# Code products of two halves in one score tile, and three PSUM banks shared by hash, transpositions and row sums

## The chip, the cores and the metric

One core of one Trainium2 chip runs the kernel. The metric is the time of one execution in device microseconds; three runs of the kernel before gave 784.03, 784.47 and 784.84 us, a median of 784.47.

## The reference

Three networks follow each other. The first is attention with a mask by hashes: batch 2, 8 heads, 768 positions, 64 columns a head, and six hash bits a position.

```
q_bits = (q @ proj > 0)            # proj: 64 x 6
k_bits = (k @ proj > 0)
mask = bucket(q_bits) == bucket(k_bits)
scores = where(mask, q @ k.T / 8, -1e9)
attn = softmax(scores)             # along the keys
x = attn @ v                       # then heads side by side: 1536 x 512
x = (sigmoid(x @ w_gate) * (x @ w_val)) @ w_out         # d_ff 1536
h = x @ w_in                                             # d_ff 2048
out = where(h >= 1, h, where(h <= -1, 0, (h + 1)^2 / 4)) @ w_out2
```

## The kernel before

The change is in the attention stage. It works on eight pairs of heads, `(b, p)`, one after the other; the two heads of a pair have `e` = 0 and 1. A pair has twelve units (6 blocks of 128 queries x 2 heads).

**A unit.** `QK` on TensorE makes 128 x 768 scores in a score tile `sc` of two PSUM banks; there are two such tiles (four banks). The mask is inside this product: beside q and k the operands hold a code of the hash bits, so a pair of another bucket gets a large negative score. Four tiles an operand, called `U`, `W`, `H` and `N` (first word of the number, rest, and the two that take codes), carry values of one head and codes of the other in their two halves of 64 partitions. `MAX` on VectorE takes the row maximum, `EXP` on ScalarE writes the probabilities `P` in SBUF and releases the score tile.

**Transpositions.** Two units give three `T`: four 128 x 128 transpositions on TensorE into one bank `pt`. `HI` (ScalarE) and `LO` (VectorE) read it out as two float16 words `PT`; `LO` releases the bank. There are two `pt` banks. `PV` multiplies `PT` by v into the bank `pv`, as two column tiles of 64, in three pieces a group of two blocks. The row sums go from `rb` through `R` (a transposition into a `pt` bank) and `RSC` (`rs`, ScalarE) into `EV`, which scales the result.

**The next pair's operands** (class `Prep`). While a pair runs, the next is prepared. GpSimd scales q and splits q and k (`SCL`, `TOP`, `RST`: tiles `U` and `W`). `Z` on TensorE makes the 24 hash products of both sides and both halves of the positions, in four groups of 32 partitions, in the bank `mm`; `BITS` (ScalarE) makes them +1 or -1 in `bt`. `XP` is a product of a code matrix with `bt`, for q or k (j) and a half of 384 positions (n): `code4[:, g]` holds the code in the 32 rows of its group and zeros in the others, so all 128 rows are used. Each of the four `XP` goes into the bank `mm`, and `H` (ScalarE, lines 406 and 408) makes codes of 384 columns in tile `N` from it. Six DMA copies an operand (`copy`, line 448, on SyncE's queue) move half tiles to the other 64 partitions; `H<-N` and `N<-W` are the last, and `N<-W` waits until `H<-N` has read `N`.

**The order** is written out as numbers. Table `AT` is for the first and the last pair and `AM` for the six between; a number is a place in units, twelve to a pair, and all steps are sorted by it and then recorded. Each engine, and SyncE's queue, takes them in that order. Tiles are taken from their pools in that order too: a step may stand only behind those that release what it takes. The weights of the gated network (`a_load`, three DMAs of 1 MB together) and their conversion to float32 have places in it as well.

The first pair has its own preparation ahead of the table (`first_round`); there the code products use 32 rows each (`part=True`). After attention the two gated networks run in one list; TensorE multiplies without a pause there.

Of the kernel before, what the change touches and what calls it, by code (L numbers as in the profile page):

```python
# [29 lines left out]
def lsh_attention_glu_act(ctx, tc, qt, kt, v, proj, w_gate, w_val, w_out1, w_in2, w_out2, ident_d, code_d, out):  # L30
# [27 lines left out]
    code4 = const.tile([128, 4, 128], BF16, name="code4")  # L58
# [3 lines left out]
    def constants():  # L62
        nc.gpsimd.memset(pz, 0.0)
        for e, r in ((0, E), (1, O)):
            nc.scalar.dma_start(pz[r, e * NB:(e + 1) * NB], proj[r])
        nc.scalar.dma_start(code, code_d)
        nc.vector.memset(bt, 0.0)
        nc.gpsimd.memset(code4, 0.0)
# [242 lines left out]
    SCB, PVB, MMB, PTB = 2, 1, 1, 2  # L311
    PB = {"pt": PTB, "pv": PVB, "mm": MMB}
# [4 lines left out]
    def bank(nm, tag):  # L317
        return pA.tile([128, 512], F32, tag=tag, bufs=PB[tag], name=nm)
# [16 lines left out]
    with ExitStack() as actx:  # L335
# [18 lines left out]
        class Prep:  # L354
# [6 lines left out]
            def part(self, n):  # L361
                return slice(0, S) if n is None else slice(n * HN, (n + 1) * HN)

            def bank(self, n, name):
                if n is None:
                    return sc_tile(name)[:, :, 0:HN]
                return pA.tile([128, 512], F32, tag="mm", bufs=MMB, name=f"{name}_{n}")[:, 0:HN]

            def sb(self, t, n):
                return v2(t) if n is None else t[:, self.part(n)]  # L370

# [9 lines left out]
            def z(self):  # L381

                self.z_ps = pA.tile([128, 512], F32, tag="mm", bufs=MMB, name=f"z_{self.b}_{self.p}")
# [53 lines left out]
            def H(self, j, n=None):  # L437
                self.x_ps = self.XB.pop((j, n))
                self.Hot(j, self.t4[j][3], slice(0, 128), n)
# [53 lines left out]
        class Flip:  # L493
            def __init__(self, n):
# [3 lines left out]
                self.ps = [None] * PCS  # L498

            def T(self, m):  # L500
                self.ps[m] = pA.tile([128, 4, 128], F32, tag="pt", bufs=PTB, name=f"pt_{self.n}_{m}")
# [79 lines left out]
        with tc.manual_schedule():  # L581
# [31 lines left out]
            load_qk(*seq[1], nc.sync)  # L613
            nc.sync.dma_start(ident, ident_d)
# [31 lines left out]
            xk = [pA.tile([128, 512], F32, tag="pt", bufs=PTB, name=f"xk_{n}")[:, 0:HN] for n in range(2)]  # L646
            for j in range(2):
                for a in range(2):
                    pp.codes(xk[a] if j else xq[:, a, 0:HN], j, a, True)
            for dst, r in ((3, E), (2, O)):  # L650
# [22 lines left out]
                "XP": (3.74, 4.91, 5.72, 7.78),  # L673
                "H": (4.54, 5.60, 7.69, 8.77),
# [12 lines left out]
                "QK": (-1.5699, -0.1016, 0.0682, 0.9466, 0.5520, 4.0360, 2.0477, 3.1663, 5.6055, 7.9530, 7.9537, 9.5136),  # L687
                "MAX": (-1.1746, 0.0191, 0.4586, 1.8498, 1.1111, 4.7351, 3.1347, 4.1102, 5.8048, 9.2404, 8.7297, 9.9059),
                "EXP": (-0.0309, 0.1949, 0.6555, 2.9824, 1.8225, 4.9578, 3.1946, 4.6720, 7.3708, 9.8795, 9.2945, 10.2827),
# [710 lines left out]
```

## Time and profile before

| | |
|---|---|
| time, median of 3 runs | 784.47 us (784.03 to 784.84) |
| time of the profiled execution | 784.46 us |
| its span | 782.7 us, 13018 instructions |
| TensorE busy | 764.4 us, 98% |
| VectorE, ScalarE, GpSimd busy | 626.5, 522.4, 169.3 us |
| mean granted clock of TensorE | 0.997 of full speed |

In the rows PE is TensorE and PEld its weight loads, DVE VectorE, ACT ScalarE, POOL GpSimd, and SPq SyncE's queue of DMAs. Busy shares are means over stages: VectorE is busy nine tenths in the first 250 us, where attention runs, and six tenths at the end. TensorE has no stage in which it is seldom busy. Matmuls are pipelined and their ends are modelled; so what one costs is read from its start to the next one's start, and a wait from the idle time in square brackets. A releaser named there is the last one that the profile saw; a DMA can have been later.

### The profile page before, as it was taken

What the parts mean: (1) busy time and instruction counts of PE and PEld (TensorE: products, weight loads), DVE (VectorE), ACT (ScalarE), POOL (GpSimd) and SP (SyncE); (2) the same over time, 40 slices, a digit from 0 to 9 for tenths busy, and PEclk for the clock granted to TensorE, in tenths of its full rate; (3) what the DMA queues carried; (4) which work ended last, traced back from release to release, by engine and by line L of the source; (5) the groups of instructions that cost most, each with busy time, mean ns of one, the idle gap of its engine ahead of it and who ended that gap; (6) DMA issues with size and microseconds to landing.
All of it is one profiled execution on the core that took longest, in us unless ns stands there. A gap on an engine that the chain in (4) does not pass through costs nothing.

```text
span 782.7 us, 13018 instructions
## 1 busy us (share of the span) xinstructions
PE 764.4 (98%) x4880; PEld 689.4 (88%) x4880; DVE 626.5 (80%) x1091; ACT 522.4 (67%) x1026; POOL 169.3 (22%) x173
## 2 busy tenths in 40 slices
PE   7999998999999999999999999999999999999997
PEld 4777876887888999999999999998998998899986
DVE  6989997989987978778769958878988867666643
ACT  6988887989875565565564544456667567766753
POOL 7656487576595000000000000000000000000000
PEclk9999999999999999999999999999999999999999
DMA  7754456354201113122122422433233201000002
GB/s 215 187 133 131 104 148 189 83 142 111 54 1 54 54 63 100 54 69 94 55 80 81 135 82 64 140 120 106 90 103 107 81 0 69 14 1 0 1 1 80
DMA packets 41391, 66.49 MB, mean 85 GB/s; under 512 B 5744, under 2 KB 28656, under 8 KB 41328
## 3 DMA queue, kind: packets, MB, share of 16 engines
q1 hardware_dynamic: 40592, 64.97, 28.4%
q8 instruction: 38, 0.62, 0.3%
q10 hardware_dynamic: 736, 0.69, 0.3%
q14 instruction: 25, 0.20, 0.1%
HBM read 45.58 MB, written 3.15 MB: 62 GB/s over the span
## 4 chain that ended last, share of the span: by engine, by line
PE 66%; DVE 1%; ACT 0%; issue 0%; ACTq 0%
PE qa L292 3%; PE qa L293 3%; PE qa L291 3%; PE p L293 3%; PE p L291 3%; PE p L292 3%; PE y L293 2%; PE qb L291 2%; PE y L292 2%; PE y L291 2%; PE qe L291 2%; PE qe L293 2%; PE qe L292 2%; PE qb L292 2%; PE qb L293 2%; PE qa L1159 2%
## 5 line engine op out<-in xcount | busy, mean ns | idle before, releaser
L517 DVE SCALAR_TENSOR_TENSOR PT<-pt,PT 128x512 f16<-128x512 f32 x144 | 95.5, 684 | 11.0 <-ACT PT L514 7.6
L478 DVE TENSOR_REDUCE st<-sc 128x1 f32<-128x768 f32 x96 | 90.9, 948 | 9.2 <-PE sc L470 8.5
L514 ACT ACTIVATE PT<-pt 128x512 f16<-128x512 f32 x144 | 81.8, 601 | 21.2 <-PE pt L505 20.3
L482 ACT ACTIVATE P<-sc,st 128x768 f32<-128x768 f32 x96 | 87.1, 908 | 8.7 <-DVE st L478 7.7
L505 PE MATMUL pt<-ident,P 128*128 128x128 f32 x576 | 80.8, 278 | 4.6 <-DVE PT L517 3.2
L505 PEld LDWEIGHTS pt<-ident,P 128*128 128x128 f32 x576 | 66.0, 141 | 14.9 <-DVE PT L517 8.2
L562 PE MATMUL O<-PT,vh 128*64 128x256 f16 x576 | 54.8, 278 | 0.0
L293 PE MATMUL p<-yh,whl_i 128*128 128x384 f32 x128 | 42.9, 336 | 0.0
L291 PE MATMUL p<-yh,whl_i 128*128 128x384 f32 x128 | 42.9, 335 | 0.0
L292 PE MATMUL p<-yl,whl_i 128*128 128x384 f32 x128 | 42.9, 335 | 0.0
L562 PEld LDWEIGHTS <-vh 128*64 128x64 f16 x576 | 30.8, 109 | 12.7 <-issue 12.5
L1136 ACT ACTIVATE t<-p,cst 128x384 f32<-128x384 f32 x32 | 18.3, 573 | 27.2 <-PE p L293 27.2
L562 PE MATMUL O<-PT,vl 128*64 128x256 f16 x288 | 34.1, 273 | 0.0
L470 PE MATMUL sc<-H,H 128*128 128x384 f32 x96 | 28.7, 380 | 3.3 <-ACT P L482 3.2
L470 PE MATMUL sc<-N,N 128*128 128x384 f32 x96 | 29.4, 387 | 1.3 <-ACT N L406 0.9
L1141 DVE SCALAR_TENSOR_TENSOR gg<-p,t 128x384 f32<-128x384 f32 x32 | 17.7, 554 | 13.4 <-ACT t L1138 13.3
L256 ACT ACTIVATE qb<-qa 128x384 f32<-128x384 f32 x24 | 11.4, 475 | 24.2 <-PE qa L293 13.5
L256 ACT ACTIVATE qd<-qb 128x384 f32<-128x384 f32 x24 | 11.4, 475 | 23.8 <-PE qb L293 20.4
L379 POOL TENSOR_TENSOR W<-n,U 128x768 fp32r<-128x768 f32 x14 | 25.5, 1824 | 0.2
L137 ACT ACTIVATE w<-wr_i 128x512 f32<-128x512 f32 x16 | 10.6, 665 | 21.8 <-DMA wr_i<-in_moe_w_in_dram 21.8
L470 PE MATMUL sc<-U,U 128*128 128x384 f32 x96 | 24.7, 338 | 0.0
L291 PEld LDWEIGHTS p<-yh,whl_i 128*128 128x128 f32 x128 | 24.0, 188 | 0.5
(1221 smaller groups left out, 2523.6 us busy)
## 6 DMA issues: line engine op xcount, KB each, us to landing
wr_o<-in_moe_w_out_dram SPq DMA_DIRECT2D x28, 512.0 KB, 3.3
H<-U SPq DMA_DIRECT2D x28, 192.0 KB, 4.0
wr_i<-in_moe_w_in_dram SPq DMA_DIRECT2D x8, 512.0 KB, 3.8
wr_i<-in_moe_w_in_dram SPq DMA_DIRECT2D x16, 256.0 KB, 3.0
n<-in_qt_dram SPq DMA_DIRECT2D x8, 384.0 KB, 4.2
n<-in_kt_dram SPq DMA_DIRECT2D x8, 384.0 KB, 5.7
vr<-in_v_dram SPq DMA_DIRECT2D x8, 384.0 KB, 3.7
wr_g<-in_moe_w_gate_dram SPq DMA_DIRECT2D x6, 512.0 KB, 3.7
```

The costliest lines, as they stand in the source:

```text
L256: nc.scalar.activation(out=self.new("bcd"[m]), in_=src, func=AF.Copy)
L291: nc.tensor.matmul(ps, lhsT=wh, rhs=rh, start=first, stop=False, **kw)
L292: nc.tensor.matmul(ps, lhsT=wh, rhs=rl, start=False, stop=False, **kw)
L293: nc.tensor.matmul(ps, lhsT=wl, rhs=rh, start=False, stop=last, **kw)
L379: nc.gpsimd.tensor_tensor(out=self.t4[j][1], in0=self.nat[j], in1=f(self.t4[j][0]), op=ALU.subtract)
L470: nc.tensor.matmul(self.sc[:, n, 0:HN], lhsT=M[:, ts], rhs=K[:, n * HN:(n + 1) * HN], start=s0, stop=not s0)
L478: nc.vector.tensor_reduce(out=self.st[:, 0, self.c:self.c + 1], in_=self.sc[:, :, 0:HN], op=ALU.max, axis=AX.XY, negate=True)
L482: nc.scalar.activation(out=self.P, in_=self.sc[:, :, 0:HN], func=AF.Exp, bias=self.st[:, 0, self.c:self.c + 1], scale=1.0, accum_out=self. ...
L505: nc.tensor.transpose(self.ps[m][:, j, :], un[2 * self.n + e].P[:, a, c:c + 128], ident)
L514: nc.scalar.activation(out=self.part(0, m), in_=self.ps[m], func=AF.Copy, scale=PSCALE)
L517: nc.vector.scalar_tensor_tensor(out=self.part(1, m), in0=self.ps[m], scalar=PSCALE, in1=self.part(0, m), op0=ALU.mult, op1=ALU.subtract)
L562: nc.tensor.matmul(O_ps[r, 0:GN], lhsT=vv[m][:, e, i * D:(i + 1) * D], rhs=PT[:, l, e * NI + i, :], start=(s == 0), stop=(s == len(steps) ...
```

## The change

- The code matrix with zeros (`code4`), its memset and its four copies on GpSimd go. `XP` uses the 32 rows of its group alone, and one step makes both halves of q or of k, each in one bank of a score tile `sc`. So `XP` and `H` are two a pair and not four, and `H` works on 768 columns.
- The bank `mm` and the two `pt` banks (now `p0` and `p1`) are one list, `free`. `Z`, `T` and `R` take the bank that was given back first; `BITS`, `LO` and `RSC` give it back. At the end of the stage the last takes are fixed, for the next stage.
- All places in `AM` are new, and those of `XP` and `H` in `AT`. The copies of the codes follow the new `H`.
- At the start the loads of the second pair's q and k and of `ident` are issued behind the copy `B<-U` of the first pair.

Of `AM` the diff shows the places of two steps.

```diff
-    code4 = const.tile([128, 4, 128], BF16, name="code4")
...
-    SCB, PVB, MMB, PTB = 2, 1, 1, 2
-    PB = {"pt": PTB, "pv": PVB, "mm": MMB}
+    SCB, PVB = 2, 1
+    two = cycle(("p0", "p1"))
+    free = ["p0", "p1", "mm"]
+
+    def take(want=None, avoid=None):
+
+        t = next(t for t in free if want in (None, t) and t != avoid)
+        free.remove(t)
+        return t
+
 
     def sc_tile(name):
         return pA.tile([128, 2, 512], F32, tag="sc", bufs=SCB, name=name)
 
     def bank(nm, tag):
-        return pA.tile([128, 512], F32, tag=tag, bufs=PB[tag], name=nm)
+        return pA.tile([128, 512], F32, tag=next(two) if tag == "pt" else tag, bufs=1, name=nm)
...
-                self.z_ps = pA.tile([128, 512], F32, tag="mm", bufs=MMB, name=f"z_{self.b}_{self.p}")
+                self.zt = take()
+                self.z_ps = bank(f"z_{self.b}_{self.p}", self.zt)
...
-            def codes(self, ps, j, n, part=False):
-
-                g = 2 * j + n
-                r = slice(ZC * g, ZC * g + ZC) if part else slice(0, 128)
-                nc.tensor.matmul(ps, lhsT=code[r] if part else code4[:, g], rhs=bt[r], start=True, stop=True)
-
-            def xp(self, j, n=None):
-                self.x_ps = self.XB[j, n] = self.bank(n, f"xp{j}_{self.b}_{self.p}")
-                for a in range(2):
-                    if n is None or n == a:
-                        self.codes(self.x_ps[:, a] if n is None else self.x_ps, j, a)
-
-            def Hot(self, j, dst, r, n=None):
-                dst = self.sb(dst, n)[r]
+                free.append(self.zt)
+
+            def codes(self, ps, j, n):
+
+                r = slice(ZC * (2 * j + n), ZC * (2 * j + n) + ZC)
+                nc.tensor.matmul(ps, lhsT=code[r], rhs=bt[r], start=True, stop=True)
+
+            def xp(self, j):
+                self.XB[j] = sc_tile(f"xp{j}_{self.b}_{self.p}")[:, :, 0:HN]
+                for n in range(2):
+                    self.codes(self.XB[j][:, n], j, n)
+
+            def Hot(self, j, dst, r):
+                dst = v2(dst)[r]
...
+                k = NU // 2 * PCS - PCS * self.n - m
+                self.bt[m] = take("p1" if k == 1 else None, "p1" if k == 2 else None)
+                self.ps[m] = bank(f"pt_{self.n}_{m}", self.bt[m]).rearrange("p (j n) -> p j n", j=4)
...
                 nc.vector.scalar_tensor_tensor(out=self.part(1, m), in0=self.ps[m], scalar=PSCALE, in1=self.part(0, m), op0=ALU.mult, op1=ALU.subtract)
+                free.append(self.bt[m])
...
-            load_qk(*seq[1], nc.sync)
-            nc.sync.dma_start(ident, ident_d)
...
-            pp, p1 = Prep(*seq[0]), Prep(*seq[1])
+            pp = Prep(*seq[0])
             pp.k2 = k2
             pp.first_round()
+            load_qk(*seq[1], nc.sync)
+            nc.sync.dma_start(ident, ident_d)
+            p1 = Prep(*seq[1])
             p1.scale()
             for j in range(2):
                 p1.top(j)
                 p1.rest(j)
-            for g in range(4):
-                r = slice(ZC * g, ZC * g + ZC)
-                nc.gpsimd.tensor_copy(code4[r, g], code[r])
...
-                "XP": (3.74, 4.91, 5.72, 7.78),
-                "H": (4.54, 5.60, 7.69, 8.77),
+                "XP": (4.404, 7.054),
+                "H": (4.70, 7.35),
...
-                "QK": (-1.5699, -0.1016, 0.0682, 0.9466, 0.5520, 4.0360, 2.0477, 3.1663, 5.6055, 7.9530, 7.9537, 9.5136),
...
-                "H": (3.0517, 4.5645, 5.3802, 8.8944),
...
+                "QK": (-1.6212, -0.3120, 0.1234, 1.0922, 0.2911, 4.4841, 2.6014, 3.1388, 4.9681, 7.5662, 8.3203, 9.8239),
...
+                "H": (6.0759, 7.8918),
...
+                w.rt = take("p1" if w.n == NU - 1 else None)
+                OB[w.n] = bank(f"r_{w.u}", w.rt).rearrange("p (j n) -> p j n", j=4)
...
+                    for j in range(2):
+                        at("XP", j, q, on, q + 1, "xp", j)
+                        at("H", j, q, on, q + 1, "H", j)
                     at("BITS", 0, q, on, q + 1, "bits")
                     at(T["TOP"][0] + 0.001 if q else -0.9, 0, q, on, q + 1, "copy", 0, 0)
                     at(T["TOP"][1] + 0.001 if q else -0.65, 0, q, on, q + 1, "copy", 1, 0)
                     for j in range(2):
                         for m in range(1, 3):
                             at(T["RST"][j] + 0.001 * m + 0.0003 * j if q else T["Z"][0] + 0.01 * m + 0.001 * j, 0, q, on, q + 1, "copy", j, m)
-                        at(T["H"][2 * j + 1] + 0.03, 0, q, on, q + 1, "copy", j, 3)
-                        at(T["H"][3] + 0.035 + 0.005 * j, 0, q, on, q + 1, "copy", j, 4)
...
+                        at(T["H"][j] + 0.03, 0, q, on, q + 1, "copy", j, 3)
+                        at(T["H"][1] + 0.035 + 0.005 * j, 0, q, on, q + 1, "copy", j, 4)
```

SyncE's queue in the fourth pair before, where the weights `wr0_v0` and `wr1_v0` are loaded; `_1_0` is the fifth pair, whose operands are prepared, `H0`, `U0` are tiles of its q and `H1`, `U1` of its k.

```order
L448 DMA W0_1_0_1327<-H0_1_0_1328 64x768
L448 DMA H0_1_0_1328<-N0_1_0_1329 64x768
L185 DMA wr0_v0_1612<-in_moe_w_val_dram 128x4x128
L187 DMA wr1_v0_1613<-in_moe_w_val_dram 128x2x128
L188 DMA wr1_v0_1613<-in_moe_w_val_dram 128x2x128
L527 DMA vrow0_95<-vm_1_0_1700 1x128x1
L448 DMA H1_1_0_1332<-N1_1_0_1333 64x768
L448 DMA N0_1_0_1329<-W0_1_0_1327 64x768
L448 DMA N1_1_0_1333<-W1_1_0_1331 64x768
```

The same place now.

```order
L443 DMA U1_1_0_1284<-W1_1_0_1285 64x768
L443 DMA W1_1_0_1285<-H1_1_0_1286 64x768
L183 DMA wr0_v0_1575<-in_moe_w_val_dram 128x4x128
L185 DMA wr1_v0_1576<-in_moe_w_val_dram 128x2x128
L186 DMA wr1_v0_1576<-in_moe_w_val_dram 128x2x128
L443 DMA H0_1_0_1282<-N0_1_0_1283 64x768
L525 DMA vrow0_93<-vm_1_0_1647 1x128x1
L443 DMA H1_1_0_1286<-N1_1_0_1287 64x768
L443 DMA N0_1_0_1283<-W0_1_0_1281 64x768
L443 DMA N1_1_0_1287<-W1_1_0_1285 64x768
```

The key's `U<-W` and `W<-H` are now the last ahead of the weight loads, and both `H<-N` stand behind them.

TensorE in the sixth pair before: a half-size code product (`xp1`: k, first half) for the seventh pair, with the score product and the transpositions behind it.

```order
L395 LDWEIGHTS code4_65
L395 MATMUL xp1_1_2_0_2527<-bt_66,code4_65 128x384
L470 MATMUL sc_1_1_0_4_2530<-H1_1_1_1783,H0_1_1_1779 128x384 x2
L470 MATMUL sc_1_1_0_4_2530<-U1_1_1_1781,U0_1_1_1777 128x384 x2
L505 MATMUL pt_31_1_2535<-ident_61,P_1_1_0_1_2345 128x128 x2
L505 MATMUL pt_31_1_2535<-ident_61,P_1_1_1_1_2430 128x128 x2
L505 MATMUL pt_32_1_2541<-ident_61,P_1_1_0_2_2403 128x128 x2
L505 MATMUL pt_32_1_2541<-ident_61,P_1_1_1_2_2511 128x128 x2
```

TensorE now, at the first of the two code products of that pair (`xp0`: q, both halves). The score tile of `sc_1_1_1_4` is the one that `xp0` took.

```order
L391 LDWEIGHTS code_64
L391 MATMUL xp0_1_2_2493<-bt_65,code_64 128x384
L391 LDWEIGHTS code_64
L391 MATMUL xp0_1_2_2493<-bt_65,code_64 128x384
L502 MATMUL pt_31_1_2497<-ident_61,P_1_1_0_1_2328 128x128 x2
L502 MATMUL pt_31_1_2497<-ident_61,P_1_1_1_1_2386 128x128 x2
L502 MATMUL pt_32_1_2508<-ident_61,P_1_1_0_2_2369 128x128 x2
L502 MATMUL pt_32_1_2508<-ident_61,P_1_1_1_2_2490 128x128 x2
L502 MATMUL pt_32_2_2513<-ident_61,P_1_1_1_2_2490 128x128 x4
L465 MATMUL sc_1_1_1_4_2530<-N1_1_1_1734,N0_1_1_1730 128x384 x2
L465 MATMUL sc_1_1_1_4_2530<-W1_1_1_1732,W0_1_1_1728 128x384 x2
```

Two products stand together now; between them and the score product that takes their tile stand twelve transpositions, where before a score product with a tile of its own followed at once.

## Rows read from the trace of the kernel before

**Rows 1.** The page, busy time and share of the span of TensorE.

```profile
PE 764.4 (98%) x4880; PEld 689.4 (88%) x4880; DVE 626.5 (80%) x1091; ACT 522.4 (67%) x1026; POOL 169.3 (22%) x173
```

**Rows 2.** Stretch, length, busy PE, PEld, DVE, ACT, POOL, granted clock, DMA share, GB/s.

```profile
42.10:68.90 26.80, 26.45 (x230) 20.84 (x222) 24.68 (x41) 24.69 (x53) 16.54 (x15) 1.00 0.48 126
68.90:97.00 28.10, 27.08 (x251) 22.06 (x246) 27.65 (x46) 24.00 (x51) 15.07 (x16) 1.00 0.49 128
97.00:129.20 32.20, 28.82 (x254) 23.23 (x246) 26.82 (x43) 24.64 (x52) 26.05 (x27) 0.95 0.56 150
129.20:156.30 27.10, 27.00 (x250) 22.09 (x246) 24.71 (x40) 24.68 (x53) 16.89 (x17) 1.00 0.47 124
...
300.00:340.00 40.00, 40.00 (x233) 40.00 (x232) 32.64 (x61) 22.60 (x45) 0.00 (x0) 1.00 0.24 75
```

**Rows 3.** Waits of TensorE in 20 to 262 us: total, times, longest.

```profile
PE pt L505 <- DVE PT L517: 2.9, 6, 1.0
...
PE pt L505 <- ACT rs L739: 0.5, 1, 0.5
```

**Rows 4.** TensorE's timeline: start, length, instruction, count, idle ahead and releaser.

```profile
75.76 0.66 PE L505 MATMUL pt<-ident,P 128*128 128x128 f32 x4 [1.02 <-DVE PT L517]
...
121.90 0.59 PE L470 MATMUL sc<-H,H 128*128 128x384 f32 x2 [2.19 <-ACT P L482]
...
122.68 1.79 PE L505 MATMUL pt<-ident,P 128*128 128x128 f32 x8
124.72 0.98 PE L470 MATMUL sc<-N,N 128*128 128x384 f32 x2 [0.26 <-DMA N<-W]
...
126.27 0.85 PE L562 MATMUL O<-PT,vh 128*64 128x256 f16 x12
```

**Rows 5.** The same view, a stretch of 2 us.

```profile
124.00:126.00 2.00, 1.74 (x7) 1.20 (x5) 0.69 (x1) 1.62 (x4) 2.00 (x3) 0.50 0.71 192
```

**Rows 6.** SyncE's queue in time: start, length, DMA.

```profile
114.62 0.59 SPq L185 DMA_DIRECT2D wr_v<-in_moe_w_val_dram  x1
...
117.01 0.55 SPq L448 DMA_DIRECT2D H<-N  x1
117.60 4.73 SPq L448 DMA_DIRECT2D N<-W  x2
```

**Rows 7.** ScalarE by shape, 20 to 240 us: count, busy, mean ns, idle before.

```profile
L482 ACT ACTIVATE P<-sc,st 128x768 f32<-128x768 f32 x92 | 83.5, 908 | 6.2 <-DVE st L478 5.2 <-DVE st L491 0.2
...
L406 ACT ACTIVATE N<-xp,cst 128x384 fp32r<-128x384 f32 x14 | 8.3, 594 | 0.1
```

**Rows 8.** Timeline of the first 22 us.

```profile
8.47 0.34 PE L395 MATMUL xq<-bt,code 32*128 32x384 bf16 x2 [0.73 <-ACT bt L389]
...
8.74 0.66 PE L619 MATMUL idle<-bt 128*128 128x384 bf16 x3
...
11.11 0.58 PE L470 MATMUL sc<-W,B 128*128 128x384 f32 x2 [0.23 <-DMA B<-U]
...
17.22 1.32 POOL L644 COPY code<-code 32x128 bf16<-32x128 bf16 x4
```

**Rows 9.** TensorE's timeline at undisturbed places.

```profile
102.09 0.34 PE L395 MATMUL xp<-bt,code 128*128 128x384 bf16 x1
102.26 0.60 PE L505 MATMUL pt<-ident,P 128*128 128x128 f32 x4
...
129.60 0.62 PE L470 MATMUL sc<-H,H 128*128 128x384 f32 x2
...
130.40 1.03 PE L505 MATMUL pt<-ident,P 128*128 128x128 f32 x8
131.19 0.59 PE L470 MATMUL sc<-N,N 128*128 128x384 f32 x2
...
139.04 1.03 PE L505 MATMUL pt<-ident,P 128*128 128x128 f32 x8
140.00 0.30 PE L562 MATMUL O<-PT,vh 128*64 128x256 f16 x2
```

More of the change, by code (lines that the diff above doesn't have):

```diff
@@ L67, in constants @@
         nc.vector.memset(bt, 0.0)
-        nc.gpsimd.memset(code4, 0.0)
         nc.vector.memset(ones, 1.0)
@@ L359, in __init__ @@
                 self.t4 = [[qtile(f"{g}{j}_{b}_{p}") for g in "UWHN"] for j in range(2)]
[L361 to L370, printed above, removed]
             def scale(self):
@@ L435, in first_even, with H @@
                 nc.vector.tensor_tensor(out=kU[E], in0=self.k2[E], in1=f(kH[E]), op=ALU.subtract)
-            def H(self, j, n=None):
-                self.x_ps = self.XB.pop((j, n))
-                self.Hot(j, self.t4[j][3], slice(0, 128), n)
+            def H(self, j):
+                self.x_ps = self.XB.pop(j)
+                self.Hot(j, self.t4[j][3], slice(0, 128))
             def rows(self, j):
@@ L497, in __init__ @@
                 self.b, self.p, self.i, self.g, self.t = u0.b, u0.p, u0.i, u0.g, u0.t
-                self.ps = [None] * PCS
+                self.ps, self.bt = [None] * PCS, [None] * PCS
             def T(self, m):
-                self.ps[m] = pA.tile([128, 4, 128], F32, tag="pt", bufs=PTB, name=f"pt_{self.n}_{m}")
+                k = NU // 2 * PCS - PCS * self.n - m
+                self.bt[m] = take("p1" if k == 1 else None, "p1" if k == 2 else None)
+                self.ps[m] = bank(f"pt_{self.n}_{m}", self.bt[m]).rearrange("p (j n) -> p j n", j=4)
                 for j in range(4):
@@ L641, in lsh_attention_glu_act @@
                 p1.rest(j)
-            for g in range(4):
-                r = slice(ZC * g, ZC * g + ZC)
-                nc.gpsimd.tensor_copy(code4[r, g], code[r])
             xq = sc_tile("xq")
-            xk = [pA.tile([128, 512], F32, tag="pt", bufs=PTB, name=f"xk_{n}")[:, 0:HN] for n in range(2)]
+            xk = [bank(f"xk_{n}", "pt")[:, 0:HN] for n in range(2)]
             for j in range(2):
                 for a in range(2):
-                    pp.codes(xk[a] if j else xq[:, a, 0:HN], j, a, True)
+                    pp.codes(xk[a] if j else xq[:, a, 0:HN], j, a)
             for dst, r in ((3, E), (2, O)):
@@ L686, in lsh_attention_glu_act @@
             AM = {
-                "QK": (-1.5699, -0.1016, 0.0682, 0.9466, 0.5520, 4.0360, 2.0477, 3.1663, 5.6055, 7.9530, 7.9537, 9.5136),
-                "MAX": (-1.1746, 0.0191, 0.4586, 1.8498, 1.1111, 4.7351, 3.1347, 4.1102, 5.8048, 9.2404, 8.7297, 9.9059),
-                "EXP": (-0.0309, 0.1949, 0.6555, 2.9824, 1.8225, 4.9578, 3.1946, 4.6720, 7.3708, 9.8795, 9.2945, 10.2827),
[9 rows of a table removed]
-                "BITS": (0.6815,),
-                "XP": (2.7247, 3.7097, 5.2725, 7.2595),
-                "H": (3.0517, 4.5645, 5.3802, 8.8944),
-                "SCL": (-0.3649,),
-                "TOP": (1.2483, -2.4969),
-                "RST": (2.2198, -0.0563),
-                "V2": (2.0470,),
-                "V3": (2.3962,),
-                "V4": (8.0690,),
-                "RB": (6.4369, 9.4375, 13.2159),
-                "VR": (7.4795,),
-                "VT": (10.7993,),
-                "STP": (3.3663, 5.9642, 10.3556),
+                "QK": (-1.6212, -0.3120, 0.1234, 1.0922, 0.2911, 4.4841, 2.6014, 3.1388, 4.9681, 7.5662, 8.3203, 9.8239),
+                "MAX": (-0.8384, -0.2820, 0.2740, 2.0221, 1.1498, 4.8574, 2.8320, 3.4570, 6.8289, 8.6318, 8.8402, 9.9223),
+                "EXP": (-0.0169, 0.1389, 0.7054, 2.7327, 1.8843, 5.1256, 3.2593, 4.9368, 7.4948, 9.0696, 9.8010, 10.9635),
[9 rows of a table added]
+                "BITS": (0.5797,),
+                "XP": (5.3627, 7.8906),
+                "H": (6.0759, 7.8918),
+                "SCL": (-2.9600,),
+                "TOP": (-0.8274, 3.4421),
+                "RST": (0.3856, 4.1980),
+                "V2": (3.2004,),
+                "V3": (4.4392,),
+                "V4": (8.6789,),
+                "RB": (7.5895, 9.9185, 12.8309),
+                "VR": (7.1203,),
+                "VT": (10.1711,),
+                "STP": (6.0380, 6.5791, 11.1927),
             }
@@ L732, in R @@
             def R(w):
-                OB[w.n] = pA.tile([128, 4, 128], F32, tag="pt", bufs=PTB, name=f"r_{w.u}")
+                w.rt = take("p1" if w.n == NU - 1 else None)
+                OB[w.n] = bank(f"r_{w.u}", w.rt).rearrange("p (j n) -> p j n", j=4)
                 for t in range(GI):
@@ L740, in RSC @@
                 RS[w.b, w.p, w.g] = rs
+                free.append(w.rt)
             def PV(w, s):
@@ L809, in lsh_attention_glu_act @@
                     at("Z", 0, q, on, q + 1, "z")
-                    for i in range(4):
-                        at("XP", i, q, on, q + 1, "xp", *divmod(i, 2))
-                        at("H", i, q, on, q + 1, "H", *divmod(i, 2))
+                    for j in range(2):
+                        at("XP", j, q, on, q + 1, "xp", j)
+                        at("H", j, q, on, q + 1, "H", j)
                     at("BITS", 0, q, on, q + 1, "bits")
@@ L818, in lsh_attention_glu_act @@
                             at(T["RST"][j] + 0.001 * m + 0.0003 * j if q else T["Z"][0] + 0.01 * m + 0.001 * j, 0, q, on, q + 1, "copy", j, m)
-                        at(T["H"][2 * j + 1] + 0.03, 0, q, on, q + 1, "copy", j, 3)
-                        at(T["H"][3] + 0.035 + 0.005 * j, 0, q, on, q + 1, "copy", j, 4)
+                        at(T["H"][j] + 0.03, 0, q, on, q + 1, "copy", j, 3)
+                        at(T["H"][1] + 0.035 + 0.005 * j, 0, q, on, q + 1, "copy", j, 4)
                         at(T["TOP"][j] + 0.002 if q else T["Z"][0] + 0.03, 0, q, on, q + 1, "copy", j, 5)
-                    at(max(T["H"][3], T["Z"][0]) + 0.06, 0, q, on, q + 1, "done")
+                    at(max(T["H"][1], T["Z"][0]) + 0.06, 0, q, on, q + 1, "done")
                 if q + 2 < NQ:
```

18 rows, old and new, of the table AM are left out of this document.

## Prediction

> **What bounds the kernel now.** I read the busy shares first: TensorE is busy 98% of the 782.7 us [rows 1], so only what shortens TensorE's list, or a wait of TensorE, can move the end. The edits all lie in the attention stage, whose end (about 240 us) hands over to a gated stage in which TensorE is never free (40.00 of 40 us in 300 to 340 [rows 2]), so a microsecond won or lost there reaches the end. The profiled execution took 784.46 us, 1.8 us more than its span; the median of the runs is 784.47, so both are one time and the sum is made against 784.46.
>
> Next the windows, cut at the hash product `z` of each pair [rows 2]: the reader is to see five periods of one and the same work that take 26.80, 28.10, 32.20 and, the fourth and fifth alike, 27.10 us. TensorE's busy time in the fourth is 27.00 of 27.10: such a period is TensorE's own list. VectorE has 24.7 there, but 27.65 of 28.10 in the second, which also carries the bit conversion of a weight. The third has 5.1 us too much. Then the waits of TensorE and its timeline with the idle time ahead of each row [rows 3, 4]. In 20 to 262 us it waited 2.9 us (6 times) for VectorE's `LO`, which frees one of the two transposition banks, and 0.5 us for the row-sum copy, which holds the same banks. The rest of the 5.1 us is one place, 119.7 to 126.3: 2.19 us idle, 0.26 us idle, and in between TensorE at the low clock (granted 0.50 in 124 to 126, the 1.2 GHz level [rows 5]), after it had stood idle 2.19 us. There eight transpositions run to 124.72 from 122.68, 2.04 us less 0.26 idle, and the next score tile runs from 124.72 to 126.27, 1.55 us, against 0.79 and 0.80 at the full clock [rows 4, 9]. So that place costs 2.19 + 0.26 + 1.0 + 0.75 = 4.2 us.
>
> Its cause: the row names an exponential that ended at about 121.0, so another wait was last, and the queue of SyncE shows it [rows 6]. Three weight loads (1 MB) are issued at 114.62, the copy `H<-N` of the next pair's operand only at 117.01, and the copies `N<-W`, which wait for it to land, stretch to 122.33. The score product that waits, `sc<-H,H` at 121.90, reads that `H`.
>
> **The change, part by part.**
>
> *Operand preparation earlier (the boundary).* Last of the next pair's four half-size code tiles was due at 8.89 of a pair's 12 units; now the second of two whole ones is due at 7.89, with the first score tile of the next pair at the same place (10.43, then 10.38). One unit is 27.1 / 12 = 2.26 us, so the copies have about 2.3 us more. Against it, both `H<-N` now stand behind the weight loads where one stood ahead. The weight loads move too: they no longer stand behind a copy that waits for ScalarE, but behind `U<-W` and `W<-H` of the keys, which GpSimd must have made. Bounds 0 to 4.2 us; I take 3.9, because an idle of 2.19 us that is met with 2.3 us of lead goes, and the 0.26 and the low clock with it.
>
> *Three banks instead of two.* Hash, transpositions and row sums now draw on three banks. What can go is the 2.9 us for `LO` and the 0.5 us for the row-sum copy: bounds 0 to 3.4. In the second period VectorE had only 0.45 us free, so of the 1.02 us wait at 75.76 less than half can go [rows 2, 4]; in the third it had 5 us free, and of the others I expect nearly all. I take 1.9.
>
> *Code products.* Before, 28 of K = 128 in 7 pairs; a product is followed after 0.17 us (102.09 to 102.26 [rows 9]). Now the two halves of a tile use 32 rows of the array each. The four of the first pair, already in that form, run together: the next instruction follows 0.27 us after the first of them (8.47 to 8.74 [rows 8]). So 14 pairs of products could win 14 x 0.17 = 2.4 us. But rows show what entering another array shape costs: eight transpositions take 0.79 us with a score tile behind them, 0.96 with a 64-column value product behind them (139.04 to 140.00) [rows 9], so 0.17 for a change of shape; each shared product adds one such change beyond those that were there, 14 x 0.17 = 2.4 us. Bounds -2.4 to +2.4 (two added changes where neither neighbour changed anyway); I take a gain of 0.6, nearer to no change. The Trainium skill, TensorEngine Tiling (Array Packing), section Tiling Modes, says that a change of the tiling mode, other than a change of tile, drains TensorE. The rows with 0.17 us bear it out; by that rule the gain would be 0, and by the concurrency alone 2.4.
>
> *Score tiles lent to the codes.* Here the change adds a wait. A shared code product takes one of the two score tiles, and the score product that takes this tile next waits for ScalarE's step on it. That step was 0.60 us on 384 columns and will be about 0.91 on 768 (the exponential of that size [rows 7]); from the product's start to the release it makes 0.34 (product [rows 8]) + 0.91 + about 0.2 for two handovers = 1.45 us. In the middle pairs twelve transpositions stand between (1.5 x 0.79 = 1.19) and the product itself (0.17): 1.36 us of cover, so 0.09 us short, 12 times: 1.0 us, with ScalarE free when the product ends. Queued behind the waiting score product are value products and the next transpositions, and ScalarE's exponentials wait for those score tiles. In the first pair one of the two has nothing between (1.3 us short) and the other eight transpositions (0.5 short): 1.8 at most. The half tiles that stood ahead of exponentials on ScalarE there go, 4 x 0.60 us, which brings the exponentials, and so the score tiles, forward by about as much as the waits put them back; I take 0.4. Together 1.4 us; bounds 0 and 14 x 0.9 = 12.6 if the cover fails.
>
> *ScalarE* saves 2 x 0.60 - 0.91 = 0.29 us a tile, 4 us in all, but is busy 24 of 27 us a period [rows 2, 7]: nothing of it on the path. GpSimd loses four copies (1.32 us [rows 8]) and a memset. The loads of the second pair and `ident` move behind the copy `B<-U`, which is now issued as soon as ScalarE has made `U`: the first score tile may wait up to 0.23 us less for it [rows 8], but its maximum stands behind work of VectorE that does not change. The moved loads land later, and GpSimd's scaling of them with it, by up to 1 us, which the 1.32 us of copies returns. Bounds -0.3 to +0.3, taken as 0.
>
> Sum: 784.46 - 3.9 - 1.9 - 0.6 + 1.4 = 779.5 us.
>
> **The rivals.**
>
> *The boundary stays.* Both copies behind the weight loads wait for the megabyte as before (the score product that reads `H` began 4.9 us after the issue of `H<-N`); the lead is spent. For it: GpSimd's list is longest in just that period (26.05 us busy [rows 2]), and the loads now wait for GpSimd. Then 779.5 + 3.9 = 783.4 us, no change that can be told.
>
> *Slower: the lent score tiles decide.* If ScalarE comes to the code tile later than TensorE has done the twelve transpositions, each of the 14 lent tiles stops TensorE by 0.9 us, and with a score ring of two the exponential behind it as well. For it: cover and chain are 1.36 against 1.45 us, no slack. Against: ScalarE has 3 us free a period. It decides from 0.5 us a tile on, where it eats the rest of the gain (14 x 0.5 = 7). At 0.9: 784.46 - 6.4 + 12.6 = 790.7 us.
>
> *More than forecast.* All `LO` waits go (3.4), the boundary too (4.2), the pairs of products win whole (2.4) and the lent tiles cost 0.6 only: 784.46 - 10.0 + 0.6 = 775.1 us. VectorE's 27.65 of 28.10 speaks against.
>
> **How the numbers follow.** The forecast, 777 to 782.5, has 0.68; the boundary that stays 0.13; slower 0.08; more than forecast 0.11. A measurement of this kernel can tell 0.2% from no change, 1.6 us: faster means under 782.9. Forecast, more, and a quarter of the boundary case lie there: 0.82. Same: 0.10. Slower: 0.08. The range that leaves out 2 in 10 is 776.3 to 783.3: it takes in most of the boundary case, and leaves out the two far ends.
>
> **What would show it.** Right: the periods from `z` to `z` are 26.6 to 27.0 us, the second about 27.5 and the third under 28; no granted clock of 0.5 near 124 us; no TensorE wait of over 0.5 us for `LO`; 32-row code products that start together. Wrong: score products that wait for the code step of ScalarE by more than 0.3 us in the middle pairs (the lent tile), the idle ahead of the fifth pair's first score tile still there (the boundary), or a value product that starts late behind a code product (the change of shape).

## Result, and the profile after

The kernel after takes 778.16 us (median of 4 runs, 776.99 to 778.95) against 784.43 us (784.03 to 784.84): ratio 0.9919, 95% interval 0.9902 to 0.9936. The forecast was 779.5 us and faster, in a range of 776.3 to 783.3. So the number was right; of the terms under it, most were not. The executions whose traces are compared here took 784.46 and 778.95 us.

The page of after: busy time and share of the span, to be held against [rows 1]. TensorE has lost 7.1 us of busy time and is still the engine without a pause.

```profile
PE 757.3 (97%) x4880; PEld 689.3 (89%) x4880; DVE 620.8 (80%) x1091; ACT 520.9 (67%) x1012; POOL 167.6 (22%) x168
```

The same five periods as in [rows 2], cut at `z` (stretch, length, busy PE, PEld, DVE, ACT, POOL, granted clock, DMA share, GB/s), and a stretch of 2 us that answers to [rows 5]:

```profile
41.19:68.09 26.90, 26.74 (x240) 21.55 (x239) 24.75 (x43) 24.84 (x53) 18.74 (x18) 1.00 0.50 132
68.09:94.73 26.64, 26.28 (x248) 22.01 (x247) 26.33 (x45) 23.55 (x50) 15.04 (x16) 1.00 0.52 135
94.73:125.38 30.65, 27.89 (x247) 23.53 (x247) 25.20 (x42) 24.52 (x52) 23.39 (x24) 0.94 0.59 158
125.38:151.43 26.05, 26.05 (x248) 21.96 (x247) 24.27 (x41) 24.31 (x51) 19.57 (x20) 1.00 0.51 130
151.43:177.47 26.04, 26.04 (x247) 21.95 (x246) 24.32 (x41) 23.49 (x50) 20.29 (x20) 1.00 0.52 137
...
120.00:122.00 2.00, 2.00 (x11) 1.90 (x10) 0.99 (x2) 0.60 (x1) 0.00 (x0) 0.50 0.81 209
```

From the starts of `z` in both timelines, the whole difference of the spans (782.67 and 777.14 us):

| stretch | before | after | difference |
|---|---|---|---|
| start to first `z` | 6.89 | 7.03 | +0.14 |
| to second `z` | 12.89 | 12.52 | -0.37 |
| to third `z` | 21.97 | 21.64 | -0.33 |
| first period | 26.77 | 26.90 | +0.13 |
| second | 28.13 | 26.64 | -1.49 |
| third (the boundary) | 32.16 | 30.65 | -1.51 |
| fourth | 27.14 | 26.05 | -1.09 |
| fifth | 27.12 | 26.05 | -1.07 |
| last `z` to the end | 599.59 | 599.66 | +0.07 |

Two things stand out. The third period is still 4.0 and 4.6 us longer than its neighbours. And the quiet fourth and fifth, in which TensorE is busy for 26.05 of 26.05 us as it was for 27.00 of 27.10, have become 1.1 us shorter: TensorE's own list takes less time.

TensorE's waits in 20 to 262 us (total, times, longest), to be held against [rows 3]:

```profile
PE sc L465 <- DMA H<-N: 2.8, 1, 2.8
PE r L732 <- POOL rb L747: 2.4, 2, 2.1
PE xp L391 <- ACT P L477: 1.3, 2, 0.9
PE sc L465 <- ACT N L403: 1.0, 1, 1.0
...
PE pt L502 <- DVE PT L514: 0.8, 2, 0.5
```

The 2.9 us for `LO` are 0.8. New are the second row, in the last pair, and the third and fourth, most of both in the first pair. The boundary in TensorE's timeline (start, length, instruction, count, idle ahead and releaser), against [rows 4]:

```profile
115.69 0.38 PE L732 MATMUL r<-ident,rb 128*128 128x128 f32 x2
118.83 0.98 PE L465 MATMUL sc<-H,H 128*128 128x384 f32 x2 [2.76 <-DMA H<-N]
119.61 0.84 PE L465 MATMUL sc<-U,U 128*128 128x384 f32 x2
120.25 2.44 PE L502 MATMUL pt<-ident,P 128*128 128x128 f32 x12
122.44 0.60 PE L465 MATMUL sc<-N,N 128*128 128x384 f32 x2
```

The idle is the stall of before, and now the row names its cause. Behind it the clock is at the 1.2 GHz level (granted 0.50 in 120 to 122): the score tile takes 1.42 us from start to start and the twelve transpositions 2.19, against 0.80 [rows 9] and 1.29 at the full clock: with the idle, 4.3 us. SyncE's queue there (start, length, DMA) answers to [rows 6]:

```profile
110.06 0.58 SPq L183 DMA_DIRECT2D wr_v<-in_moe_w_val_dram  x1
...
111.91 0.47 SPq L443 DMA_DIRECT2D H<-N  x1
...
113.12 0.96 SPq L443 DMA_DIRECT2D H<-N  x1
118.15 1.10 SPq L443 DMA_DIRECT2D N<-W  x2
```

Both `H<-N` come right behind the megabyte of weights. In 104 to 124 us the DMA view gives them (KB each, median us from issue to landing)

```profile
U<-W SPq DMA_DIRECT2D x2, 192.0 KB, 2.6
H<-N SPq DMA_DIRECT2D x2, 192.0 KB, 5.8
N<-W SPq DMA_DIRECT2D x2, 192.0 KB, 2.9
```

5.8 us to land, where copies of the same size just before and after them took 2.6 and 2.9. One by one, the last 256 KB of the weights, issued at 111.29, take 6.3 us and land at 117.6; the two `H<-N` take 6.2 and 5.5 and land at 118.1 and 118.6.

### The profile page after: what moved, and what is told of

It reads as the page before. It is cut to its first block, busy times and chain, and to the rows that moved or that the text cites. A ratio compares the mean times of both kernels' runs of the same rounds, so it can differ in the third digit from the quotient of the medians.

```text
span 777.1 us, 12993 instructions
## 1 busy us (share of the span) xinstructions
PE 757.3 (97%) x4880; PEld 689.3 (89%) x4880; DVE 620.8 (80%) x1091; ACT 520.9 (67%) x1012; POOL 167.6 (22%) x168
## 4 chain that ended last, share of the span: by engine, by line
PE 67%; DVE 1%; ACT 0%; issue 0%; ACTq 0%
PE qa L289 3%; PE qa L291 3%; PE qa L290 3%; PE p L291 3%; PE p L289 3%; PE p L290 3%; PE qb L289 2%; PE y L289 2%; PE y L291 2%; PE qe L289 2%; PE y L290 2%; PE qe L291 2%; PE qe L290 2%; PE qb L291 2%; PE qb L290 2%; PE qa L1157 2%
## 5 line engine op out<-in xcount | busy, mean ns | idle before, releaser
L502 PE MATMUL pt<-ident,P 128*128 128x128 f32 x576 | 78.9, 278 | 0.8 <-DVE PT L514 0.8
L1134 ACT ACTIVATE t<-p,cst 128x384 f32<-128x384 f32 x32 | 18.3, 573 | 27.1 <-PE p L291 27.1
```

Of the source, the lines that this page charges most:

```text
L502: nc.tensor.transpose(self.ps[m][:, j, :], un[2 * self.n + e].P[:, a, c:c + 128], ident)
```

## Experiments

Before these, my theory was: the boundary is the weight load; the last pair's wait is GpSimd's list; the steady gain is TensorE's list, with fewer changes of array shape. The rivals: the copies are slow of themselves; GpSimd has no time to give; the steady gain is the third bank, or the 32-row products. Times are medians with the ratio to the kernel before on the same chip and its 95% interval; "the changed kernel" has 0.9919.

**The weight load behind the copies (a_load).**

```
-   a_load("v0")                      # in first_weights, place 4.8 of the fourth pair
+   at(8.0, 0, 3, a_load, "v0")       # behind the last N<-W of that pair
```

> The changed kernel (778.2 us), with one edit: the 1 MB load of the next layer's weights goes on SyncE's queue behind the fourth pair's last copies of code rows instead of right ahead of the two H<-N. Theory 'the weight load holds the copies': H<-N lands within 2 us of its issue, the idle of 2.76 us before the fifth pair's first score tile goes, and with it the stretch at half clock behind it (12 transpositions in 2.44 us, against 1.47 at full clock: 1.0 us); 774.5 to 775.0 us, period of the fourth pair 30.65 to about 26.9. Rival 'the copies are slow of themselves, or the score tile is awaited for something else': the idle stays, 778.2 within 0.7. A third way: the weights now run against the fifth pair's own copies and a new idle of 1 to 2 us stands in the fifth pair: 776 to 777.

774.71 us, 0.9878 (0.9863 to 0.9892). The period of the boundary and the next one:

```profile
94.14:120.18 26.04, 26.04 (x247) 21.95 (x247) 24.83 (x42) 24.15 (x51) 21.84 (x23) 1.00 0.64 170
120.18:146.23 26.05, 26.05 (x248) 21.96 (x247) 24.33 (x41) 24.40 (x52) 21.01 (x21) 1.00 0.58 146
```

and the landing of the copies:

```profile
H<-N SPq DMA_DIRECT2D x2, 192.0 KB, 2.9
```

`H<-N` lands in half the time, the idle and the low clock are gone, 30.65 became 26.04: the weight load ahead of the copies is shown as the cause. The copies `H<-U`, which now stand behind the weights, take 4.5 us to land in place of 3.0; no wait for them came in the fifth pair. Whether the order of the queue holds the copies, or DMA engines that the weights keep busy (DMA share 1.02 and 1.09 in 112 to 114 and 114 to 116 us of the changed kernel), is not told apart.

**The same edit in the kernel before (b_load).**

> The kernel before (784.4 us), with one edit: the same weight load moved behind the fourth pair's last copies. Theory 'the stall ahead of the fifth pair has the same cause in both kernels, and the changed kernel's order did not touch it': the idles of 2.19 and 0.26 us and the slow stretch around them go, the fourth pair's period falls from 32.16 to about 28, 780.5. Rival 'before, the score tile waited for EXP, as the row of that wait says': the stall stays, 784.4 within 0.7.

781.81 us, 0.9972 (0.9957 to 0.9988). In the profile no wait is left at the boundary:

```profile
68.43:98.43 30.00, 27.40 (x248) 22.18 (x247) 27.95 (x45) 24.15 (x51) 16.96 (x18) 1.00 0.48 120
98.43:127.06 28.63, 27.03 (x247) 22.07 (x247) 27.01 (x42) 24.61 (x52) 19.81 (x21) 1.00 0.60 157
127.06:155.98 28.92, 27.54 (x247) 22.19 (x247) 24.73 (x41) 24.93 (x53) 21.79 (x22) 1.00 0.51 129
```

The third period fell from 32.16 to 28.63; the fourth rose by 1.8, with new waits for `EV` (0.63 us) and `N<-W` (0.65 us). The second is 1.9 longer too, though nothing was edited there, with waits for the copies `H<-N` (0.71) and `N<-W` (0.91) ahead of the fourth pair; with the same places and the load where it was it is 29.92 in the profile of b_banks, so the moved load need not be the reason. This execution took 784.52 us, of 780.36 to 784.67, and gave back all that it won. So the cause at the boundary was the same in both kernels; why the fourth period rose is not shown.

**The third bank alone (b_banks).** The kernel before, with its own places:

```
-   tag="pt", bufs=2   (T, R)         tag="mm", bufs=1   (Z, XP)
+   take() from ["p0", "p1", "mm"] for Z, XP, T and R; free.append behind BITS, H, LO and RSC
```

> The kernel before (784.4 us), with its own places and its own code products, and one edit: transpositions, row sums, hash products and half code products take any of three single banks instead of two for transpositions and row sums and one for the rest. Theory as forecast 'the bank waits are a term of their own, 1.9 us': waits of transpositions for LO fall from 2.9 and 0.5 to under 1, 782.5. Rival 'the third bank is worth nothing without new places': the single bank's users take turns with the transpositions, waits only move, 784.4 within 0.7. Rival 'the bank is more than forecast', since short waits under the view's bound also go (0.26 us a pair): 781.

783.65 us, 0.9990 (0.9981 to 0.9999). `LO` is awaited as long as before:

```profile
PE pt L518 <- DVE PT L530: 3.2, 4, 1.7
```

The fourth and fifth periods are 27.42 and 27.11 us, against 27.14 and 27.12. A third bank without new places gives 0.9 us in the median and nothing in a quiet period. Here the four half code products of a pair still draw on the three banks, which in the changed kernel they do not; the run leaves open what the third bank is worth without them.

**The 32-row form undone (a_code4).**

```
-   nc.tensor.matmul(ps, lhsT=code[r], rhs=bt[r], ...)
+   nc.tensor.matmul(ps, lhsT=code4[:, g], rhs=bt, ...)     # 128 rows; copies of code4 at the start
```

> The changed kernel (778.2 us), with one part undone: the code products run over 128 rows with zeros around the code (and four GpSimd copies at the start that make that operand), in the places and tiles of the changed kernel. Theory 'as forecast, the 32-row form is worth 0.6 us': the two products of a tile start 0.16 apart instead of 0.003, and the next transposition comes 0.17 behind them instead of 0.26, so 0.07 more each time, 0.14 a pair, 1 us in all: 779.1, period 26.05 to 26.2. Rival 'the step into and out of the 32-row shape eats it': 778.2, period unchanged. Rival 'it carries the steady gain': period about 27, 784.

780.09 us, 0.9950 (0.9935 to 0.9966), but the period says what the form is worth: 26.07 and 26.09 against 26.05. The profiled execution (784.25 us, the longest of 778.71 to 784.25) has 5.4 us more span than the changed kernel's: 2.7 at the boundary, where TensorE waited 4.7 us for `H<-N`, 1.6 behind the last `z`, where its clock was 0.91 in 220 to 240 us, 0.6 ahead of the first, and 0.3 between the first and the third. What the 1.9 us of the medians are is not shown; the form's share of them, by the period, is small. A code tile and what follows, in this kernel:

```profile
166.95 0.50 PE L393 MATMUL xp<-bt,code 128*128 128x384 bf16 x2
167.29 1.47 PE L504 MATMUL pt<-ident,P 128*128 128x128 f32 x12
168.51 0.59 PE L467 MATMUL sc<-N,N 128*128 128x384 f32 x2
```

and in the changed one:

```profile
163.22 0.33 PE L391 MATMUL xp<-bt,code 32*128 32x384 bf16 x2
163.48 1.53 PE L502 MATMUL pt<-ident,P 128*128 128x128 f32 x12
164.77 0.60 PE L465 MATMUL sc<-N,N 128*128 128x384 f32 x2
```

From the code product to the next score product it is 1.56 and 1.55 us. The two 32-row products do run together (the next row follows after 0.26 us, not 0.34), and the transpositions behind them take 1.29 instead of 1.22: the change of shape eats the gain.

**More entries into value products (a_split).**

```
-   "PV": (9.4781, 9.7900, ..., 16.1918, ..., 19.7470)
+   "PV": (9.4781, 9.8240, ..., 16.4842, ..., 19.8907)     # and EV 16.3989 to 16.4843
```

> The changed kernel (778.2 us), with three value-product pieces of each middle pair moved by one instruction group, so that a pair of score products (twice) or of code products (once) stands between pieces that stood together: TensorE enters value products 9 times a pair instead of 6. Theory 'a change of array shape has a price of its own': from start-to-start steps of the changed kernel's trace, a score product between two pieces costs 0.202 + 0.267 + 0.204 against 0.053 + 0.202 + 0.177, 0.24 more, and a code product 0.16 more; 0.64 a pair, period 26.05 to 26.7, 6 pairs 3.8 us: 782.0. Rival 'the steps between shapes only fill time in which another engine is the bound': period 26.05, 778.2 within 0.7.

783.62 us, 0.9998 (0.9986 to 1.0010); the fifth period is 27.47, 1.42 more. One place of it:

```profile
158.77 0.30 PE L560 MATMUL O<-PT,vh 128*64 128x256 f16 x2
...
159.54 0.62 PE L465 MATMUL sc<-N,N 128*128 128x384 f32 x2
...
160.44 0.85 PE L560 MATMUL O<-PT,vh 128*64 128x256 f16 x12
161.22 1.09 PE L502 MATMUL pt<-ident,P 128*128 128x128 f32 x8
```

From the first piece to the transpositions it takes 2.45 us. In the changed kernel, with the two pieces together, the same work takes 2.24 us (158.54 to 160.78):

```profile
158.54 0.30 PE L560 MATMUL O<-PT,vh 128*64 128x256 f16 x2
...
159.22 0.82 PE L560 MATMUL O<-PT,vh 128*64 128x256 f16 x12
159.97 0.61 PE L465 MATMUL sc<-N,N 128*128 128x384 f32 x2
...
160.78 1.03 PE L502 MATMUL pt<-ident,P 128*128 128x128 f32 x8
```

TensorE is busy throughout both (2.45 of 2.45 and 2.24 of 2.24 us). So an entry costs about 0.2 us. The rest of the 1.42 is a wait of 0.58 us for an exponential, elsewhere in the period, and some 0.2 that I can't place. The direction and the price of a shape are shown; the total, forecast as 3.8 us and measured as 5.5, was under-estimated. In the profile 3.9 us of it stand behind the last `z`, where the clock was 0.83 in 219 to 229 us, and the third period is 3.0 shorter, without the idle for `H<-N`.

**Fewer entries (a_merge).**

```
-   "PV": (..., 13.8068, 15.5835, ..., 17.0135, 19.6520, ...)
+   "PV": (..., 15.5834, 15.5835, ..., 19.6519, 19.6520, ...)
```

> The changed kernel (778.2 us), with two numbers of the middle pairs' table changed: the first value-product piece of the second and of the third group is put right ahead of the group's second piece, so that TensorE enters value products 4 times a pair instead of 6. Theory 'the steady gain is fewer changes of array shape': from steps in the trace of the changed kernel, a piece that stands alone costs 0.267 + 0.203 at its two ends, against 0.177 + 0.055 without it, so 0.24 less each: 2 x 6 x 0.24 = 2.9 us, period 26.05 to about 25.6, 775.3. Rival 'the places were set by what is ready when': TensorE comes 0.7 us sooner to transpositions and score tiles that wait for EXP or for a bank, and the saving turns into waits: 778.2 or up to 3 us more.

783.81 us, 0.9984 (0.9973 to 0.9996): 5.6 us slower than the changed kernel, so the rival came, and stronger than its 3 us. The value products of a period did fall (6.63 to 6.38 us of steps), and TensorE then stood for ScalarE, in the fifth period twice:

```profile
155.77 0.62 PE L465 MATMUL sc<-H,H 128*128 128x384 f32 x2 [0.23 <-ACT P L477]
163.42 0.34 PE L391 MATMUL xp<-bt,code 32*128 32x384 bf16 x2 [0.54 <-ACT P L477]
```

The second is the code product, which waits until an exponential gives back a score tile. The places are a balance between shapes and what is ready.

**The last pair (a_xop).** In the changed kernel GpSimd makes `rb` behind other work (start, length, instruction):

```profile
215.54 0.83 POOL L124 CAST hB<-xr 128x768 fp32r<-128x768 f32 x1
216.45 1.80 POOL L104 TENSOR_TENSOR lB<-xr,hB 128x768 fp32r<-128x768 f32 x1
218.20 0.40 POOL L747 COPY rb<-st 128x256 f32<-128x256 f32 x1
```

```
-   ("lB21", 5.0), ("hB22", 5.1), ("lB22", 5.2)        # RB stands at 5.4
+   ("lB21", 5.41), ("hB22", 5.42), ("lB22", 5.43)
```

> The changed kernel (778.2 us), with one edit: in the last pair three GpSimd operations on the dense layers' operands (about 4.5 us together: two subtractions of 1.8, a copy of 0.8) go behind the copy that makes the row-sum operand rb, instead of ahead of it. Theory 'GpSimd's list now holds TensorE there': rb comes at 213.8 instead of 218.2, the 2.07 us wait of the row-sum transposition goes, and 2.0 us of time with it: 776.2. Rival 'GpSimd is full to the pair's end, so the same work is only late elsewhere': the wait turns up at the next rb or at the first dense products, 778.2 within 0.7.

775.29 us, 0.9881 (0.9868 to 0.9894). From the last `z` to the end it takes 597.56 instead of 599.66 us: the 2.1 us came, and no later wait took them. The remaining 0.8 of the median is not this edit's to claim: its third period, 29.22 us, had a shorter idle for `H<-N` (2.0 us).

**Both (a_best).**

> The changed kernel (778.2 us) with both edits that shortened it: the weight load behind the fourth pair's last copies (774.7 alone) and the three GpSimd operations of the last pair behind rb (775.3 alone, of which the profile shows 2.1 in the last pair and the rest in the varying landing of H<-N). Theory 'two separate waits, so the gains add': 778.2 - 3.5 - 2.1 = 772.6. Rival 'TensorE comes 4.6 us sooner to a last pair in which GpSimd's list is full, so a wait for it opens again': 774 to 775.

772.13 us, 0.9852 (0.9838 to 0.9867), and last `z` to end 597.50: the gains add. This version beats both kernels.

**The first pair (a_first, a_first2).** On top of it:

```
-   "XP": (4.404, 7.054), "H": (4.70, 7.35)
+   "XP": (5.035, 7.054), "H": (5.04, 7.35)                                     # a_first
+   "XP": (5.035, 7.87), "H": (5.04, 7.88), and one EXP from 8.14 to 7.86       # a_first2
```

> The shortest kernel so far (the changed kernel with the weight load and the three GpSimd operations moved, 772.1 us), with the first pair's first code product and its threshold step put behind the next score tile instead of ahead of two transpositions. Theory 'the score tile lent in the first pair costs TensorE and ScalarE an idle, and two transpositions could stand in it': the 0.94 us idle ahead of the code product goes, ScalarE's 0.43 idle with it, first pair 21.65 to 20.8 to 21.2: 771.5. Rival 'ScalarE is the bound of the first pair, which has about 1 us free in 13': the idle only moves to the score tile or to a transposition, 772.1 within 0.5.

> As the last one, and the first pair's second code product goes behind the score tile that waited 0.99 us for its threshold step, with one EXP drawn ahead of a bank's eviction to make room (the table is also that of the last pair, where only this EXP moves). Theory 'the second idle goes too': 771.5 - 0.9 = 770.6. Rival 'the code rows then come about 1.4 us later, and their copies land behind the second pair's first score products': the saving is lost there, 771.5 to 773.

772.80 us, 0.9846 (0.9828 to 0.9864), and 774.25 us, 0.9868 (0.9855 to 0.9882). In the first the stretch to the third `z` is 21.47 instead of 21.65, with the idle still there (25.53, 0.90 us for `EXP`); in the second it is 23.20, and the waits of TensorE there are now

```profile
PE xp L391 <- ACT P L477: 1.8, 2, 0.9
PE pt L502 <- ACT rs L735: 1.2, 1, 1.2
```

All name ScalarE, not the late copies. I read from it that ScalarE's chain is the bound there and that the idles of the lent tiles only mark it; no run takes work from ScalarE to test it.

**The order of loads at the start (a_start).** The loads of the second pair and of `ident` ahead of the first round again, in the shortest kernel:

> The shortest kernel so far (772.1 us), with one part of the change undone: at the start the second pair's queries and keys and the identity are loaded ahead of the first round, as before, instead of behind its one copy of code rows. Theory as forecast 'the order of loads at the start is worth nothing': 772.1 within 0.5, the first score tile at the same distance from the first hash products. Rival 'the copy then waits behind 0.8 MB of loads, and the first scores are later': 772.5 to 774.

772.72 us, 0.9849 (0.9833 to 0.9866): the same by the time. But its profile has, in the first scores and in the second pair's,

```profile
11.55 0.59 PE L465 MATMUL sc<-W,B 128*128 128x384 f32 x2 [0.64 <-DMA B<-U]
...
39.49 0.59 PE L465 MATMUL sc<-N,N 128*128 128x384 f32 x2 [0.97 <-DMA N<-W]
```

two idles that the profile of the shortest kernel does not have; from first to third `z` it takes 35.50 us, against 34.16. That one in turn lost 1.5 us at the boundary, with 0.5 us of wait for `N<-W` among it (27.53 against 26.05), which this execution did not. So between these two executions the order is worth up to 1.3 us in its place; the medians do not show it.

## Why the prediction was right, and where it was not

**The view of what bounds** held: TensorE's list and its waits, and the place of 4.2 us at 119.7 to 126.3.

**Boundary, -3.9: failed.** Two steps are wrong. The first is "the copies have about 2.3 us more": it reads places as times, and a place gives only the order. The last code step of the keys on ScalarE (start, length), before and after:

```profile
114.49 0.59 ACT L408 ACTIVATE N<-xp,cst 128x384 fp32r<-128x384 f32 x1
```

```profile
110.75 0.90 ACT L403 ACTIVATE N<-xp,cst 128x768 fp32r<-128x768 f32 x1 [0.61 <-PE xp L391]
```

From its end to the moment at which TensorE could begin the score product that waits it is 4.6 us before (115.08 to 119.71) and 4.4 after (111.65 to 116.07): no lead was won. a_load and b_load have 4.2 and 4.4 us there and no wait, so this much was enough in both kernels, once no load stood ahead. The second wrong step is "an idle of 2.19 us that is met with 2.3 us of lead goes": the queries' `H<-N` now stood behind the weights as well, and both copies took 5.8 us to land. The place at 119.7 to 126.3 cost 4.2 us, and the same place after 4.3; by the period it is 5.0 (32.16 - 27.14) and 4.6 (30.65 - 26.05). The paragraph on the rival had this to the letter, with a chance of 0.13. What was misjudged is the kind of wait: in this trace a copy queued behind a megabyte landed 0.5 and 1.0 us after the last of the weights, so time gained by TensorE, in earlier pairs too, turned into idle. a_split and a_merge, in which TensorE comes there later, show no such idle.

**Three banks, -1.9: the waits went, not for the reason given.** `LO` fell from 2.9 to 0.8 us and the row-sum copy's wait went; the second period, "about 27.5", became 26.64. By b_banks the bank alone gives none of that. It needs the new places, or banks without the code products; no run tells these two apart.

**Code products, -0.6: the size was off**, measured 0.01 us a tile. The Trainium skill, TensorEngine Tiling (Array Packing), section Tiling Modes, says that a change of the tiling mode drains TensorE. The trace agrees with the gain of 0 that the forecast took from that: 1.55 us with the 32-row form and 1.56 without it.

**Lent score tiles, +1.4: too dear.** In the middle pairs no wait of a score product for the code step is listed. In the first pair the chain can be read where nothing covers it:

```profile
28.60 0.34 PE L391 MATMUL xp<-bt,code 32*128 32x384 bf16 x2
...
28.98 0.90 ACT L403 ACTIVATE N<-xp,cst 128x768 fp32r<-128x768 f32 x1 [0.43 <-PE xp L391]
...
29.93 0.62 PE L465 MATMUL sc<-N,N 128*128 128x384 f32 x2 [0.99 <-ACT N L403]
```

It is 1.33 us and not 1.45: the two handovers, taken as 0.2 with no row for them, are 0.09 together. Product and twelve transpositions, taken as 1.36, cover 1.55. So there are 0.2 us of slack where the sum had 0.09 us too little, and the slower rival, which rested on that, was out of reach. In the first pair this idle came, 0.99 us of the 1.3; the one behind eight transpositions, taken as 0.5, is at most 0.27 (1.06 us for transpositions that take 0.79). The other listed idles, 0.94 us in the first pair and 0.36 in the third, stand ahead of a code product that waits for an exponential to give back a score tile, which the sum did not hold; the idle of a_merge is of that kind too. Yet the stretch to the third `z` is 0.33 shorter.

**Start, 0:** first to second `z` -0.37, outside the bounds of 0.3; the 0.23 us for `B<-U` went. But this stretch took 12.52 to 12.95 us in the profiles with the new order of loads and 12.70 to 13.49 in those with the old one, so the 0.37 is not shown to be the order's. The first `z` was 0.14 later, which varies between executions (5.91 to 7.63 us).

**What the sum did not hold: the quiet periods, -1.1 each.** I had taken a period of 27.1 us in which TensorE is always busy as fixed but for the code products. From start to start in the fifth period: transpositions 8.11 to 7.51 us, row sums 0.81 to 0.49, value products 6.88 to 6.63, code products 0.65 to 0.53, score products 9.89 to 10.11. The new places enter value products 6 times instead of 8, and always from a score product, never from a transposition, a code product or a row sum. Before, one group of eight transpositions took 1.11 us (161.59 to 162.70) where eight take 0.79, in short waits that the view of waits does not list (the weight loads for them waited 0.33 us for `LO`); b_banks has the same 1.11, and in the changed kernel's fifth period no group loses more than 0.1. b_banks and a_code4 exclude bank and 32-row form as its cause by themselves. By a_split's price two entries fewer are some 0.4 of the 1.1, and that one group 0.3. The split is worked out from steps, not tested apart, and that the code products left the single banks was not undone in any run: its share stays open.

**And the last pair, +2.1**, was in no term: TensorE came earlier to a row sum whose operand is GpSimd's. Before, `rb` was ready at 225.11 us and TensorE took it at 225.49. Counted from the last `z`, GpSimd finished it 0.9 us earlier after the change and TensorE was ready for it 3.3 us earlier.

So -3.9 was missing, about -1.1 in each quiet period and more in the second stood in for it, and the sum came out by compensation: the number was right by luck.

## What to carry to other kernels

A place in a list is an order and not a time, so a lead is to be read from the trace. And a lead of 4.4 us did not help small copies that were queued right behind a megabyte: look at what stands ahead of them on the queue; here moving the load paid. When an engine is always busy its list is still not fixed: the order of its instructions has a price, read from start to start at places where shapes change. And when the bound engine gets faster, go through what each of its later waits hangs on, since the next list in line (here GpSimd's) was just in time only for the old pace.

## What the runs showed of the hardware

A change between value products of 64 columns and other shapes costs TensorE about 0.2 us a visit (2.45 against 2.24 us), with TensorE shown busy throughout. In the changed kernel, in 104 to 124 us, copies of 192 KB took 2.5 to 3.0 us to land with no load right ahead of them, and 6.2 and 5.5 behind a megabyte of weights; behind the loads of v, q and k, at 101 us, they took 5.8. The wait for `H<-N` varied between three kernels with the same order of loads there: 2.0, 2.8 and 4.7 us. Idles of TensorE in one and the same place were followed by different clocks: behind 2.07 us in the last pair of the changed kernel the granted clock was 1.00 throughout (216 to 226 us, the 2.4 GHz level); behind 1.79 us in a_split it was 0.50 in 223 to 225 us, the 1.2 GHz level.
